# The first three token blocks of a linear-attention and double-MLP kernel in one written order on all engines

## The chip, the cores and the metric

The kernel runs on one core of a Trainium2 chip. The metric is the time of one execution in microseconds on the device. A core has TensorE (PE; PEld is its weight load), VectorE (DVE), ScalarE (ACT), GpSimd (POOL) and SyncE (SP), each with its own queue of instructions that it executes in order. Here SP issues the DMA transfers. A granted clock of 1.00 in the tables is 2.4 GHz on TensorE.

## What is computed

Three layers follow one another: chunked linear attention with decay over 4 sequences of 768 positions and 8 heads, a gated MLP (256 to 1536 to 256) and a second MLP with h times sigmoid(h) (256 to 2048 to 256). The inputs of the MLPs' weights are float64.

```python
for c in range(nc):
    cum = np.cumsum(la, axis=-1)
    L = np.exp(cum[:, :, :, None] - cum[:, :, None, :]) * causal
    M = np.einsum('bhin,bhjn->bhij', Cc, Bc) * L
    y_intra = np.einsum('bhij,bhjd->bhid', M, xc)
    y_inter = np.einsum('bhin,bhnd->bhid', Cc, state) * decay_to_i[:, :, :, None]
    y[:, :, sl] = y_intra + y_inter
    state = decay_full[:, :, None, None] * state + np.sum(Bx, axis=2)
...
gate = 1.0 / (1.0 + np.exp(-(x @ w_gate)))
x1 = gate * (x @ w_val) @ w_out
h = x1 @ w_in
out = (h * (1.0 / (1.0 + np.exp(-h)))) @ w_out2
```

## The kernel before

The 3072 tokens are 24 chunks of 128 positions. A chunk q is sequence q // 6 and place q % 6 (divmod with NCH), so chunks of one sequence stand one behind the other, and each needs the state S of the chunk ahead. The chunks are gathered into seven token blocks, BLOCKS = [2, 2, 4, 4, 4, 4, 4], and the first MLP works block by block.

For a chunk, L is a tile of 128 x 1024 (eight heads) of decays. It is loaded by a DMA that spreads one row over the partitions (at_loadL, L212; for chunk 0 straight from the input, L210) and turned into products of decays by a scan on VectorE (at_L, L295). B and C are loaded as bc; for the first NX = 4 chunks TensorE transposes them (at_wide1), for later ones bf16 pieces are made on GpSimd (L255, L263), ScalarE and VectorE (L280) and transposed by DMA (L284). at_cb multiplies them into PSUM and VectorE takes the product with L (L337). at_y multiplies by x and adds the state's part, at_state and at_state2 (L377, L389) carry the state on with bw (L303) and cw (L308) from GpSimd, and at_yT splits the result into a high and a low part xT (L404, L405).

Weights come as float64, read as pairs of int32. For each of the twelve blocks f of 128 hidden columns, load_w fetches gate, value and output weights (256 KB each), and conv makes float32 out of them: two passes on ScalarE (L136, L137), two on VectorE (L138, L139), an add on GpSimd (L146), then a high part on ScalarE (L147) and a remainder on VectorE (L148). For f < NAT = 7 w_out is first kept whole in a spare place of x1T (L144), used so by the first two blocks, and split later (w1_split, L181 and L182).

A tick (b, f) is a gate product (six matmuls, L462), a sigmoid on ScalarE (L475), a value product (six matmuls), its product with the gate on VectorE (L483) and the output step (L511). In blocks 0 and 1 with f < 7 the output step is two plain float32 products with the whole w_out; everywhere else the gated value is split first (gh on ScalarE, L456; gl on VectorE, L492) and the step has six matmuls. The gate and value products share three PSUM banks (tag gv).

SP's order is written by hand (manual_schedule). The order of the other engines comes from the scheduler of the framework, which simulates the program in the order in which the steps are emitted: slot_steps lists one chunk's steps, and the loop over the ticks mixes them in at an even rate. In the first two blocks the ticks go by groups of GRP = 3 weight blocks, block 0 and block 1 in turn. LAG = 2 output steps stay behind the ticks, across the ends of blocks too. Behind the first MLP follows the second one (L715 to L766), which the change leaves alone but for the rows of the output.

## Time and profile before

| | |
|---|---|
| median of 3 runs (lowest to highest) | 680.84 us (679.74 to 682.12) |
| the profiled execution, its own time | 681.07 us |
| its span, first to last instruction | 679.4 us |
| busy: PE, DVE, ACT, POOL | 647.1, 435.9, 329.3, 106.2 us |
| mean granted TensorE clock | 0.987 |

The times say how long an execution took; the span leaves out what lies around the program's instructions, 1.7 us here. Busy is the time in which an engine executed something, waits that lie inside an instruction among it. The shares over the whole span hide that the stretches differ: the page's row of 40 slices (17 us each) shows PE below 90% in six of the first seven slices and at 90% or more in all but the last of those behind.

### The profile page before, as it was taken

The page shows a single profiled execution, that of the slowest core. Times are in us where ns is not written, and L with a number is a line of the kernel's source. Part 1 is how long each engine was busy: PE and PEld are TensorE (multiplying, and loading weights), DVE is VectorE, ACT ScalarE, POOL GpSimd, SP SyncE. Part 2 cuts the span into 40 slices and gives each one's busy share as a digit, 9 for nine tenths or more (in the row PEclk, how much of TensorE's full clock was granted, in tenths as well). Part 3 has the DMA queues.
Part 4 walks back from the last instruction along what each step waited for, and adds up shares of the span by engine and source line. Part 5 has one row for each costly group of instructions (what it writes and reads, how often), then busy time and mean ns, then how long its engine had stood idle before and what let it go on. Part 6 is the DMA issues. An engine that isn't in the chain of part 4 may idle for free.

```text
span 679.4 us, 10006 instructions
## 1 busy us (share of the span) xinstructions
PE 647.1 (95%) x3728; PEld 524.6 (77%) x3728; DVE 435.9 (64%) x658; ACT 329.3 (48%) x647; POOL 106.2 (16%) x128
## 2 busy tenths in 40 slices
PE   5689788999999999999999999999999999999997
PEld 2368676777777777777787888888888888888887
DVE  8887987766766858656699345464464555644544
ACT  5576634444343644435476334453454444544443
POOL 4545612212121313111133000000000000000000
PEclk9889989999999999999999999999999999999999
DMA  8936568767566375533132000000000000000000
GB/s 204 266 111 182 118 121 152 154 141 129 96 111 141 69 154 119 99 81 116 50 123 77 1 0 1 1 22 10 1 32 1 1 31 1 31 1 1 32 1 31
DMA packets 140144, 51.18 MB, mean 75 GB/s; under 512 B 119008, under 2 KB 133536, under 8 KB 140096
## 3 DMA queue, kind: packets, MB, share of 16 engines
q1 hardware_dynamic: 140096, 50.55, 32.5%
q8 instruction: 29, 0.48, 0.3%
q14 instruction: 19, 0.16, 0.1%
HBM read 36.80 MB, written 3.24 MB: 59 GB/s over the span
## 4 chain that ended last, share of the span: by engine, by line
PE 79%; DVE 7%; DMA 3%; issue 2%; POOL 1%; ACT 1%; SPq 1%; DVEq 0%; ACTq 0%; POOLq 0%
PE h L462 20%; PE acc L511 12%; PE v L462 12%; PE g L462 11%; PE o L740 11%; PE o L751 7%; PE o L746 2%; PE y L352 2%; PE cb L335 1%; DMA raw<-in_moe_w_out_dram 1%; DMA L<-ac_d 1%; DVE cvt L139 1%; DVE L L295 1%; PE y L346 1%; POOL cvt L146 1%
## 5 line engine op out<-in xcount | busy, mean ns | idle before, releaser
L462 PE MATMUL g<-xT,w 128*128 128x512 f32 (+1 forms) x504 | 123.3, 375 | 4.2 <-DVE sg L483 3.8
L462 PE MATMUL v<-xT,w 128*128 128x512 f32 (+1 forms) x504 | 121.6, 373 | 0.2 <-ACT sg L475 0.2
L462 PE MATMUL h<-x2T,w2b 128*128 128x512 f32 x432 | 113.3, 395 | 0.0
L720 DVE TENSOR_TENSOR sh<-h,sh 128x512 f32<-128x512 f32 x96 | 66.4, 691 | 69.5 <-ACT sh L719 69.0
L462 PEld LDWEIGHTS g<-xT,w 128*128 128x128 f32 x504 | 87.7, 191 | 23.4 <-DVE sg L483 4.8
L725 DVE TENSOR_TENSOR gl<-sh,gh 128x512 fp32r<-128x512 f32 x96 | 66.0, 691 | 55.4 <-ACT gh L456 31.8
L462 PEld LDWEIGHTS v<-xT,w 128*128 128x128 f32 x504 | 87.5, 192 | 16.9 <-issue 1.0
L511 PE MATMUL acc<-gh,w 128*128 128x512 f32 (+1 forms) x280 | 96.0, 385 | 1.3 <-ACT x1T L519 1.3
L719 ACT ACTIVATE sh<-h 128x512 f32<-128x512 f32 x96 | 57.7, 601 | 80.7 <-PE h L462 76.1
L456 ACT CAST gh<-sh 128x512 fp32r<-128x512 f32 x96 | 59.2, 620 | 60.1 <-DVE sh L720 53.8
L462 PEld LDWEIGHTS h<-x2T,w2b 128*128 128x128 f32 x432 | 76.5, 188 | 15.2
L456 ACT CAST gh<-sg 128x512 fp32r<-128x512 f32 (+1 forms) x70 | 41.2, 588 | 86.5 <-DVE sg L483 86.4
L740 PE MATMUL o<-w2b,gh 128*128 128x512 f32 x240 | 75.4, 395 | 0.0
L483 DVE TENSOR_TENSOR sg<-v,sg 128x512 f32<-128x512 f32 (+1 forms) x84 | 51.0, 607 | 32.1 <-PE v L462 31.4
L492 DVE TENSOR_TENSOR gl<-sg,gh 128x512 fp32r<-128x512 f32 (+1 forms) x70 | 49.5, 708 | 28.6 <-ACT gh L456 28.3
L475 ACT ACTIVATE sg<-g 128x512 f32<-128x512 f32 (+1 forms) x84 | 45.0, 536 | 37.8 <-PE g L462 34.7
L295 DVE TENSOR_TENSOR_SCAN L<-L,eye 128x1024 f32<-128x1024 f32 x24 | 55.5, 2313 | 10.7 <-DMA L<-ac_d 10.6
L511 PEld LDWEIGHTS acc<-gh,w 128*128 128x128 f32 x280 | 52.5, 191 | 12.6 <-ACT x1T L519 1.8
L751 PE MATMUL o<-w2b,gl 128*128 128x256 f32 x288 | 60.1, 280 | 0.0
L511 PE MATMUL acc<-gl,w 128*128 128x512 f32 (+1 forms) x140 | 54.1, 386 | 4.3 <-DVE gl L492 4.3
L146 POOL TENSOR_TENSOR cvt<-cvt,raw 128x512 int32<-128x512 int32 (+1 forms) x28 | 46.5, 1662 | 67.5 <-DVE cvt L139 47.8
L751 PEld LDWEIGHTS o<-w2b,gl 128*128 128x128 f32 x288 | 49.1, 188 | 4.9
(94 smaller groups left out, 782.0 us busy)
## 6 DMA issues: line engine op xcount, KB each, us to landing
L<-ac_d SPq DMA_DIRECT2D x23, 512.0 KB, 4.6
raw<-in_moe_w_out_dram SPq DMA_DIRECT2D x28, 256.0 KB, 3.6
raw<-in_moe_w_in_dram SPq DMA_DIRECT2D x16, 256.0 KB, 2.7
x<-in_x_dram SPq DMA_DIRECT2D x24, 128.0 KB, 3.0
raw<-in_moe_w_gate_dram SPq DMA_DIRECT2D x12, 256.0 KB, 4.2
raw<-in_moe_w_val_dram SPq DMA_DIRECT2D x12, 256.0 KB, 4.6
out_dram<-o2t SPq DMA_DIRECT2D x24, 128.0 KB, 1.8
bc<-in_B_dram SPq DMA_DIRECT2D x24, 64.0 KB, 2.7
```

Source lines behind the costliest of these rows:

```text
L146: nc.gpsimd.tensor_tensor(ti, ti, r, ALU.add)
L295: nc.vector.tensor_tensor_scan(t["Lf"], t["Lf"], eye, 0.0, op0=ALU.mult, op1=ALU.add)
L456: nc.scalar.copy(hi[:, :n], sg[:, :n])
L462: nc.tensor.matmul(psum[:, :n], w[:, i, o + k * P : o + (k + 1) * P], xt[j][:, k, :n], start=(z == 0), stop=(z == len(k_terms) - 1),)
L483: nc.vector.tensor_mul(sg[:, :n], ps[:, :n], sg[:, :n])
L492: nc.vector.tensor_sub(lo[:, :n], sg[:, :n], hi[:, :n].bitcast(F32))
L511: nc.tensor.matmul(o, v[:, ms], g[:, :n], start=(f == 0 and z == 0 and not (small and m)), stop=(f == NF1 - 1 and z == len(terms) - 1), sk ...
L719: nc.scalar.activation(sg, ps, AF.Sigmoid)
L720: nc.vector.tensor_mul(sg, ps, sg)
L725: nc.vector.tensor_sub(lo, sg, hi.bitcast(F32))
L740: nc.tensor.matmul(ps, hi[:, s], w2(f)[:, :, DM:], start=(f == 0), stop=False, skip_group_check=True,)
L751: nc.tensor.matmul(ps[:, :DM], lo[:, s], w2(f)[:, 0, DM:], start=False, stop=(f == NF2 - 1), skip_group_check=True,)
```

## The change

Chunks are numbered by their place in the sequence: place(q) gives sequence q % 4 and place q // 4, so chunks 0 to 3 are the starts of the four sequences and chunk q takes the state of chunk q - 4. Each sequence has a state tile S2 of its own, and the rows of the output follow the new numbers.

Everything up to the end of block 2 is cut into 657 named steps (a chunk's loads, transposes, scan, products and state; a weight block's seven conversion steps; a tick's five or seven), and a string ORDER lists them. They are emitted in that order with manual_schedule on PE, ACT, DVE and POOL as on SP before. Behind them the scheduler is free again; block 3 begins with no output step left over from block 2. The names: ldw, Af, Ar, D, G, Go, h, l, sh, sl are the weight block's steps, g, sig, v, mul, out (ghi, glo) the tick's, with block and f.

The decays of chunks 0 and 1 no longer come by DMA: all 32 rows' first 128 values are split into two float32r parts, a_hl, and TensorE multiplies them by a column of zeros and ones spread over 128 columns, so that one row lands on all partitions in PSUM (16 matmuls); the scan reads PSUM in two halves.

All twelve weight blocks keep w_out whole for blocks 0 and 1 (SPARE), so no gated value of these two blocks is split. Staging has 3 raw and 3 cvt buffers in place of 4 and 2, bw 2 in place of 1, S 4 in place of 2.

```diff
-NAT = 7
-GRP = 3
+NB = 2
...
+ORDER = """
+aload ldbc.0 ldx.0 aprep ldw.1 arest tp.0 ldL.0 bT.0 dec1 cT1.0 ldw.0 ldL.1 cT0.0 L.0 ldbc.1 Ar.1 cp0.0 ldx.3
...
+cwa.12 ldx.14 cm0.12 cp1.12 cm1.12 st.12 ss.12
+"""
...
-    stg = {"n": 768, "raw": 4, "cvt": 2, "p": sstack.enter_context(tc.tile_pool(name="stg1", bufs=1))}
+    stg = {"n": 768, "raw": 3, "cvt": 3, "p": sstack.enter_context(tc.tile_pool(name="stg1", bufs=1))}
...
+    def place(q):
+
+        return q % nb, q // nb
...
+        steps = [
+            lambda: nc.scalar.activation(f, v[:, :, 1].bitcast(F32), AF.Copy, scale=2.0**-112),
+            lambda: nc.scalar.activation(r, v[:, :, 0].bitcast(U32), AF.Copy, scale=2.0**-29),
+            shift,
+            lambda: nc.gpsimd.tensor_tensor(ti[:, :m], ti[:, :m], r[:, :m], ALU.add),
+            lambda: nc.scalar.copy(hi, f[:, :m]),
+            lambda: nc.vector.tensor_sub(lo, f[:, :m], hi.bitcast(F32)),
+        ]
         if whole is not None:
-            n -= whole.shape[-1]
...
+            steps.append(lambda: nc.gpsimd.tensor_tensor(whole.bitcast(I32), ti[:, m:], r[:, m:], ALU.add))
+        return steps
...
-    whole = lambda f: x1T[0][:, f % 2, NT - (f // 2 + 1) * DM : NT - f // 2 * DM]
...
+    SPARE = [(0, 2048), (1, 2048), (0, 512), (0, 768), (1, 512), (1, 768)]
+    SPARE += [(0, 1024), (0, 1280), (1, 1024), (1, 1280), (0, 1536), (0, 1792)]
+    whole = lambda f: x1T[0][:, SPARE[f][0], SPARE[f][1] : SPARE[f][1] + DM]
...
     def at_loadL(q):
-        b, c = divmod(q, NCH)
+        b, c = place(q)
         t = T[q]
         sl = slice(c * L, (c + 1) * L)
         t["Lf"] = ap_.tile([P, H * L], F32, tag="L", name=f"L{q}", bufs=LB)
         t["L"] = t["Lf"].rearrange("p (h l) -> p h l", h=H)
-        if q == 0:
-            nc.sync.dma_start(out=t["L"], in_=a[b, :, sl].unsqueeze(0).to_broadcast([P, H, L]))
-        else:
-            nc.sync.dma_start(out=t["Lf"], in_=ac_d[c : c + 1, b].to_broadcast([P, H * L]))
+        if q < NB:
+
+            if q == 0:
+                two = ps_acc.tile([P, KM, 512], F32, tag="acc", name=f"a{q}")
+                t["a"] = [two[:, 0], two[:, 1]]
+            else:
+                t["a"] = [ps_at.tile([P, 512], F32, tag=g, name=f"a{q}{g}") for g in ("misc", "cb")]
+            for h in range(H):
+                nc.tensor.matmul(
+                    t["a"][h // 4][:, h % 4 * L : (h % 4 + 1) * L],
+                    pick[:, b * H + h : b * H + h + 1].to_broadcast([2 * U, P]), a_hl,
+                    start=True, stop=True, skip_group_check=True,
+                )
+            return
+        nc.sync.dma_start(
+            out=t["Lf"], in_=ac_d[c : c + 1, b].to_broadcast([P, H * L])
+        )
...
+    def at_L(q):
...
+        if q >= NB:
+            nc.vector.tensor_tensor_scan(t["Lf"], t["Lf"], eye, 0.0, op0=ALU.mult, op1=ALU.add)
             return
...
+        for i in range(2):
+            hs = slice(i * 512, (i + 1) * 512)
+            nc.vector.tensor_tensor_scan(
+                t["Lf"][:, hs], t["a"][i], eye[:, hs], 0.0, op0=ALU.mult, op1=ALU.add
+            )
...
-            if q % NCH:
+            if q >= nb:
                 for m in range(KM):
                     nc.tensor.matmul(
-                        t["y"][:, m], T[q - 1]["S"][:, m * P : (m + 1) * P], t["cwT"],
+                        t["y"][:, m], T[q - nb]["S"][:, m * P : (m + 1) * P], t["cwT"],
...
-    S2 = ap_.tile([P, 2 * D], F32, name="S2")
...
+    S2 = [ap_.tile([P, 2 * D], F32, name=f"S2_{b}") for b in range(nb)]
...
-        add(s + 1, at_state2)
+        add(s - 2, at_state2)
...
-        if b < 2 and f < NAT:
...
+        if b < 2:
...
-        if b >= 2 or f >= NAT:
...
+        if b >= 2 and hi:
+            m1_hi(b, f)
...
+    order = ExitStack()
+    order.enter_context(
+        tc.manual_schedule(
+            engines={
+                mybir.EngineType.PE, mybir.EngineType.Activation,
+                mybir.EngineType.DVE, mybir.EngineType.Pool,
+            }
+        )
+    )
...
+    pick = ap_.tile([2 * U, U], F32R, name="pick")
+    a_hl = ap_.tile([2 * U, L], F32R, name="a_hl")
...
+    def a_prep():
+        clip(a_sb[:, :L])
+        nc.vector.tensor_copy(first[:, 0:1], a_sb[:U, 0:1])
+        nc.vector.memset(a_sb[:, 0:1], 0.0)
+        nc.vector.tensor_copy(a_hl, a_sb[:, :L])
+        nc.vector.tensor_sub(a_hl[U:], a_sb[U:, :L], a_hl[U:].bitcast(F32))
...
+    for k in ORDER.split():
+        plan.pop(k)["fn"]()
+    assert not plan, list(plan)
+    order.close()
...
-            r = b * 512 + t * P
+            i, c = place(b * 4 + t)
+            r = i * S + c * L
...
```

Three places of the order. First VectorE at the start: before, from the clip of chunk 0's decays on (L0, L1 are the decay tiles, cb the products of B and C, cvt and raw a weight block in conversion, e_i and dec the decays for the states).

```order
L201 TENSOR_SCALAR L0_112<-L0_112 128x1024
L558 COPY e_i_155<-ps_e_156 128x192
L295 SCALAR_TENSOR_TENSOR L0_112<-L0_112,eye_97 128x1024
L337 TENSOR_TENSOR L0_112<-cb0_0_164,L0_112 128x512
L567 TENSOR_TENSOR dtmp_197<-ps_e_156,blk_93 128x192
L573 TENSOR_REDUCE dec_199<-dtmp_197 128x24
L138 TENSOR_SCALAR cvt3_201<-cvt3_201 128x768
L139 SCALAR_TENSOR_TENSOR cvt3_201<-raw1_121,cvt3_201 128x768
L337 TENSOR_TENSOR L0_112<-cb0_1_167,L0_112 128x512
L375 COPY S2_104<-st0_188 128x64
L295 SCALAR_TENSOR_TENSOR L1_128<-L1_128,eye_97 128x1024
```

VectorE at the same place after the change, from the scan of the 32 rows for the states on (a0, a1misc and a1cb are the spread decays in PSUM).

```order
L738 SCALAR_TENSOR_TENSOR x1T_81<-x1T_81 32x768
L393 SCALAR_TENSOR_TENSOR L0_141<-a0_142,eye_97 128x512 x2
L393 SCALAR_TENSOR_TENSOR L1_162<-a1misc_163,eye_97 128x512
L393 SCALAR_TENSOR_TENSOR L1_162<-a1cb_164,eye_97 128x512
L186 TENSOR_SCALAR cvt4_192<-cvt4_192 128x768
L187 SCALAR_TENSOR_TENSOR cvt4_192<-raw2_158,cvt4_192 128x768
L459 TENSOR_TENSOR L0_141<-cb0_1_198,L0_141 128x512
L459 TENSOR_TENSOR L0_141<-cb0_0_184,L0_141 128x512
L186 TENSOR_SCALAR cvt3_182<-cvt3_182 128x768
L187 SCALAR_TENSOR_TENSOR cvt3_182<-raw1_131,cvt3_182 128x768
```

The scans of chunks 0 and 1 stand one behind the other now, ahead of the first weight conversion, and the second conversion follows the first with only two products between.

Then ScalarE between chunk 1's transposes and the results of the first two chunks (xT0 is the high part of a result y, w1 the converted weights): before, where the second weight block's conversion stands behind the first result.

```order
L243 COPY bT1_173<-bcT1_170 128x128
L247 ACTIVATE x1T_81<-bcT1_170,blk_93 128x128 x8
L404 CAST xT0_0_243<-y0_231 128x2x128
L319 COPY cwT1_249<-cwT1_247 128x128
L181 CAST w1_103<-x1T_81 128x256
L147 CAST w1_103<-cvt3_201 128x512
L136 ACTIVATE cvt5_281<-raw2_132 128x768
L137 ACTIVATE raw2_132<-raw2_132 128x768
L404 CAST xT0_0_243<-y1_259 128x2x128
```

ScalarE at the same place after the change.

```order
L321 COPY bT1_224<-bcT1_214 128x128
L328 ACTIVATE x1T_81<-bcT1_214,blk_93 128x128 x8
L193 ACTIVATE raw5_217<-raw5_217 128x768
L192 ACTIVATE cvt6_253<-raw5_217 128x768
L542 CAST xT0_0_274<-y0_232 128x2x128
L196 CAST w1_103<-cvt3_182 128x512
L196 CAST w1_103<-cvt4_192 128x512
L542 CAST xT0_0_274<-y1_291 128x2x128
```

The conversion of the third weight block (raw5) moved ahead of both results and of the high parts of the first two weight blocks.

Last VectorE in block 2, ticks 2 and 3 (sg the gated values, gl their remainders, L9 to L14 decay tiles of later chunks): before.

```order
L483 TENSOR_TENSOR sg2_2_1502<-v2_2_1512,sg2_2_1502 128x512
L280 COPY st010_1457<-bc310_1442 128x8x32
L280 COPY st110_1475<-bc310_1442 128x8x2x16
L295 SCALAR_TENSOR_TENSOR L10_1065<-L10_1065,eye_97 128x1024
L337 TENSOR_TENSOR L9_972<-cb9_0_1396,L9_972 128x512
L377 SCALAR_TENSOR_TENSOR S2_104<-S2_104,dec_199,st9_1489 128x64
L405 TENSOR_TENSOR xT1_3_1454<-y8_1402,xT0_3_1453 128x2x128
L492 TENSOR_TENSOR gl2_2_1521<-sg2_2_1502,gh2_2_1520 128x512
L389 TENSOR_TENSOR S9_1504<-S2_104,blk_93 128x256
L483 TENSOR_TENSOR sg2_3_1572<-v2_3_1577,sg2_3_1572 128x512
```

VectorE there after the change, from the product of tick 1 on.

```order
L642 TENSOR_TENSOR sg2_1_1390<-v2_1_1397,sg2_1_1390 128x512
L363 COPY st110_1410<-bc310_1356 128x8x2x16
L654 TENSOR_TENSOR gl2_1_1424<-sg2_1_1390,gh2_1_1423 128x512
L389 SCALAR_TENSOR_TENSOR L9_1408<-L9_1408,eye_97 128x1024
L363 COPY st010_1438<-bc310_1356 128x8x32
L389 SCALAR_TENSOR_TENSOR L10_1426<-L10_1426,eye_97 128x1024
L642 TENSOR_TENSOR sg2_2_1436<-v2_2_1429,sg2_2_1436 128x512
L389 SCALAR_TENSOR_TENSOR L14_1442<-L14_1442,eye_97 128x1024
L514 SCALAR_TENSOR_TENSOR S2_1_105<-S2_1_105,dec_116,st9_1464 128x64
L389 SCALAR_TENSOR_TENSOR L11_1459<-L11_1459,eye_97 128x1024
L514 SCALAR_TENSOR_TENSOR S2_0_104<-S2_0_104,dec_116,st8_1497 128x64
L642 TENSOR_TENSOR sg2_3_1469<-v2_3_1471,sg2_3_1469 128x512
```

Where one scan stood between two ticks, four stand between tick 1 and tick 3, and the scan of chunk 14, which the list does not hold, was set among them by the scheduler.

## Rows read from the trace of the kernel before

**Rows 1.** Windows by stage: busy us (instructions) per engine, granted clock, DMA share, GB/s.

```profile
0.00:26.40 26.40, 15.11 (x89) 7.19 (x89) 22.23 (x32) 15.70 (x41) 10.23 (x22) 0.90 0.86 209
26.40:119.50 93.10, 77.24 (x610) 64.99 (x608) 77.00 (x116) 50.75 (x114) 38.37 (x36) 0.94 0.65 152
119.50:181.00 61.50, 61.50 (x381) 46.95 (x381) 42.83 (x67) 28.55 (x62) 13.57 (x24) 0.99 0.70 134
181.00:679.40 498.40, 493.29 (x2655) 405.50 (x2653) 293.81 (x445) 234.32 (x431) 44.00 (x47) 1.00 0.19 47
```

**Rows 2.** VectorE's waits, 26.4 to 119.5 us: us in total, times, longest.

```profile
DVE cvt L138 <- ACT cvt L136: 3.4, 3, 2.1
```

**Rows 3.** VectorE's groups, 26.4 to 119.5 us: busy us, mean ns | idle before.

```profile
L483 DVE TENSOR_TENSOR sg<-v,sg 128x256 f32<-128x256 f32 x24 | 10.0, 415 | 2.0 <-PE v L462 2.0
L337 DVE TENSOR_TENSOR L<-cb,L 128x512 f32<-128x512 f32 x12 | 8.2, 684 | 3.8 <-PE cb L329 3.0 <-PE cb L335 0.8
...
L182 DVE TENSOR_TENSOR w<-x1T,w 128x256 fp32r<-128x256 f32 x6 | 6.2, 1027 | 0.0
L148 DVE TENSOR_TENSOR w<-cvt,w 128x512 fp32r<-128x512 f32 x6 | 5.1, 850 | 0.4 <-ACT w L147 0.4
...
L405 DVE TENSOR_TENSOR xT<-y,xT 128x256 fp32r<-128x256 f32 x6 | 2.5, 419 | 0.7 <-ACT xT L404 0.7
L377 DVE SCALAR_TENSOR_TENSOR S<-S,dec,st 128x64 f32<-128x64 f32 x4 | 1.1, 277 | 1.6 <-PE st L368 1.6
```

**Rows 4.** Lines of VectorE, 0 to 190 us: shortest/median/longest ns, first and last start.

```profile
L138 DVE TENSOR_SCALAR cvt<-cvt x12: 545/552/1178, 11.9 to 81.1; 128x768 int32<-128x768 int32 x12
L139 DVE SCALAR_TENSOR_TENSOR cvt<-raw,cvt x12: 942/955/1158, 12.5 to 83.1; 128x768 int32<-128x768 int32 x12
L148 DVE TENSOR_TENSOR w<-cvt,w x12: 681/943/2335, 20.0 to 90.8; 128x512 fp32r<-128x512 f32 x7, 128x768 fp32r<-128x768 f32 x5
L182 DVE TENSOR_TENSOR w<-x1T,w x7: 416/892/1525, 19.1 to 57.5; 128x256 fp32r<-128x256 f32 x7
L389 DVE TENSOR_TENSOR S<-S,blk x12: 400/424/1458, 16.4 to 186.7; 128x256 f32<-128x256 f32 x12
L280 DVE COPY st<-bc x24: 194/220/1877, 72.1 to 180.4; 128x256 bf16<-128x256 bf16 x24
```

**Rows 5.** Timeline near 30 us: start, duration in us, engine, line.

```profile
30.24 2.28 DVE L295 TENSOR_TENSOR_SCAN L<-L,eye 128x1024 f32<-128x1024 f32 x1
...
30.45 2.59 POOL L144 TENSOR_TENSOR x1T<-cvt,raw 128x256 int32<-128x256 int32 x1 [2.34 <-DMA raw<-in_moe_w_out_dram]
...
33.01 1.48 POOL L146 TENSOR_TENSOR cvt<-cvt,raw 128x512 int32<-128x512 int32 x1
```

**Rows 6.** Lines of GpSimd, 0 to 190 us: shortest/median/longest ns.

```profile
L144 POOL TENSOR_TENSOR x1T<-cvt,raw x7: 727/927/2594, 13.6 to 56.3; 128x256 int32<-128x256 int32 x7
...
L255 POOL TENSOR_TENSOR bcr<-bc x12: 614/615/1422, 69.0 to 178.4; 128x256 f32<-128x256 f32 x12
...
L303 POOL TENSOR_TENSOR bw<-bc,L x13: 412/446/1180, 10.2 to 184.2; 128x128 f32<-128x128 f32 x13
```

**Rows 7.** Timeline of the opening: first weight conversion, an f32 product, the first gate's run.

```profile
10.60 0.91 ACT L136 ACTIVATE cvt<-raw 128x768 f32<-128x768 f32 x1 [3.06 <-DMA raw<-in_moe_w_out_dram]
...
25.29 2.07 PE L329 MATMUL cb<-x1T,bT 128*128 128x512 f32 x2
...
26.37 1.98 PE L462 MATMUL g<-xT,w 128*128 128x256 f32 x5
```

**Rows 8.** TensorE's timeline: tick 11 of block 2, first gates of blocks 3 and 4.

```profile
172.97 1.56 PE L462 MATMUL g<-xT,w 128*128 128x512 f32 x6
174.37 1.56 PE L462 MATMUL v<-xT,w 128*128 128x512 f32 x6
...
178.19 1.65 PE L462 MATMUL g<-xT,w 128*128 128x512 f32 x6
...
237.34 1.65 PE L462 MATMUL g<-xT,w 128*128 128x512 f32 x6
```

More of the change, by code (lines that the diff above doesn't have):

```diff
@@ L228, in at_load_x @@
     def at_load_x(q):
-        b, c = divmod(q, NCH)
+        b, c = place(q)
         t = T[q]
@@ L398, in at_yT, with at_yT_lo, x_alloc @@
         if i == 0:
+            x_alloc(b)
+        nc.scalar.copy(xT[b][0][:, :, i * L : (i + 1) * L], t["y"])
+    def at_yT_lo(q):
+        b, i = blk_of[q]
+        hi, lo = (v[:, :, i * L : (i + 1) * L] for v in xT[b])
+        nc.vector.tensor_sub(lo, T[q]["y"], hi.bitcast(F32))
+    def x_alloc(b):
+        if b != 1:
             xT[b] = [
@@ L515, in m1_out, with m1_x1 @@
                 )
-        if f == NF1 - 1:
-            for m in range(KM):
-                o = a_[:, m * n : (m + 1) * n] if small else a_[:, m, :n]
-                nc.scalar.copy(x1T[0][:, m, start_of[b] : start_of[b] + n], o)
+        if f == NF1 - 1 and to_x1:
+            m1_x1(b)
+    def m1_x1(b):
+        n = BLOCKS[b] * L
+        small = n <= 256
+        a_ = acc[b - b % 2][:, b % 2] if small else acc[b]
+        for m in range(KM):
+            o = a_[:, m * n : (m + 1) * n] if small else a_[:, m, :n]
+            nc.scalar.copy(x1T[0][:, m, start_of[b] : start_of[b] + n], o)
@@ L607, in tile_linattn_moe_moe @@
-    ticks = [(b, f) for fs in GR for b in (0, 1) for f in fs]
-    seen.add(("w", 0))
-    seen.add(("x", 0))
-    for b in range(2, len(BLOCKS)):
-        ticks += [(b, f) for f in range(NF1)]
+    scr = lambda k, i, n=U: x1T[0][:n, k, i * S : (i + 1) * S]
+    order = ExitStack()
[5 more added lines that the diff above has]
+            }
+        )
+    )
@@ new lines, in decays1, with decays2, decays3, decays4 @@
+    def decays1():
+        nc.vector.tensor_tensor_scan(first, a_sb[:U], first, 0.0, op0=ALU.mult, op1=ALU.add)
+    def decays2():
+        T[0]["e"] = ps = ps_at.tile([P, 512], F32, tag="misc", name="ps_e")
+        for c in range(NCH):
+            nc.tensor.transpose(
+                ps[:, c * U : (c + 1) * U], first[:, c * L : (c + 1) * L], ident[:U, :U]
+            )
+    def decays3():
+        nc.vector.tensor_copy(e_i.rearrange("p c u -> p (c u)"), T[0]["e"][:, : NCH * U])
+    def decays4():
+        T[0]["d"] = ps = ps_at.tile([P, 512], F32, tag="misc", name="ps_d")
+        nc.tensor.matmul(
+            ps[:, : NCH * U], sel, e_i.rearrange("p c u -> p (c u)"), start=True, stop=True
+        )
@@ L613, in tile_linattn_moe_moe @@
+    step("dec4", "PE", 0.64, decays4, after=["dec3"], takes=[("misc", 1, ["dec5"])], lag=0.2, group="d")
+    step("dec5", "DVE", 0.72, decays5, after=["dec4"], lock=True, group="d")
+    for q in range(ends[PB] + 3):
+        plan_chunk(q, 5 if q < ends[PB] else 2 - q + ends[PB])
+    for f in range(NF1):
+        plan_weights(f)
+    for b in range(PB):
+        for f in range(NF1):
+            plan_tick(b, f)
+    ticks = [(b, f) for b in range(PB, len(BLOCKS)) for f in range(NF1)]
     w2st = {}
@@ L616, in run @@
         for _ in range(min(k, len(steps))):
-            steps.pop(0)()
-    def need(k):
-        while k not in seen:
             steps.pop(0)()
```

532 lines of the change are left out of this document (354 added, 178 removed).

## The prediction

> **What bounds the kernel now.** I read the windows by stage first. The trace falls into four stretches [rows 1]: an opening up to 26.4 us, the first two token blocks up to 119.5 us, the third block up to 181.0 us, and the rest. In the third block TensorE is busy for all of its 61.50 us and in the rest for 493.29 of 498.40 us, so there nothing but less matmul work would help. The second stretch is different: TensorE has 77.24 us of work in 93.10 us, and VectorE is busy for 77.00 us. So the order can gain in one place: what the 93.1 us are made of.
>
> VectorE's time there has three parts. The groups of lines [rows 3] and the shortest durations [rows 4] give the first two. With the groups that read SBUF twice at their shortest duration and the others, of fourteen, at their mean, count by count, VectorE needs 62.9 us (for instance 6 x 0.416 us for the w_out remainder at L182 that took 6.2 us, 6 x 0.681 us for L148 that took 5.1 us). The other 14.1 us of its 77.0 busy us are stretch. The last 16.1 us are idle, put down to other engines' late results; the largest is a wait for a weight conversion on ScalarE [rows 2].
>
> The stretch has a visible cause. In rows 5 a scan on VectorE starts at 30.24 us and a GpSimd add starts 0.21 us later; the add ends at 33.04 us, 0.52 us after the scan, though such an add takes 0.73 us otherwise [rows 6]. On VectorE the operations with two SBUF inputs reach up to nine times their shortest duration (L182 1.525 for 0.416, L280 1.877 for 0.194) [rows 4], while L337 and L483, which read PSUM, keep 684 and 415 ns as means [rows 3]. So the two engines take turns wherever VectorE reads SBUF twice, and about 0.2 us of a turn is hidden at the hand-over.
>
> **The opening: no gain.** The decays of the first two chunks are now spread by TensorE instead of by DMA. That is 16 matmuls of 128 columns. No row shows this form. Bounds: 0.06 us each, a quarter of the 0.23 us that a 512-column one takes in rows 8, and 0.26 us, a quarter of the f32 product at 25.29 us (2.07 us for two) [rows 7]. That is 1 to 4 us in all; I take 2.5. VectorE has the clips and a 32-row scan to do meanwhile, so it is covered. The scans of chunks 0 and 1 can then run one behind the other from about 6.5 us.
>
> What holds the first gate is data. The weight conversion in rows 7 starts on ScalarE at 10.60 us, when the DMA lands, and 1.77 MB were issued up to that transfer. In the new order of SP the second weight block issued (f = 0, the first one used), the third and x of chunk 1 stand at 2.03, 3.57 and 4.23 MB (weight blocks of 0.79 MB, L tiles of 0.52, x and bc of 0.13 each, a and its copy of 0.10). With the 209 GB/s of the opening [rows 1] they land 1.2, 8.6 and 11.8 us later, at 11.8, 19.2 and 22.4 us. On ScalarE the two conversions of the third block (0.91 us each) stand ahead of the small copies that the first gate needs, as the order of ScalarE above shows: 19.2 + 1.8 + about 1.6 for three copies, an estimate of half a conversion each, is 22.6 us. VectorE then does one remainder (0.68), the scan of chunk 2 (2.28) and two short ones (0.7): 26.3 us. Before, the first gate's run begins at 26.37 us [rows 7]. I put both at 26.4.
>
> **The first two blocks: the term that decides.** In the new order VectorE has, between the first gate and the first gate of block 2, 10 conversions (0.545 + 0.942), 6 scans (2.28), 12 products with the decays (0.684), 11 remainders (0.681), 24 value products (0.415), 11 remainders of w_out (0.416), 12 copies for the transposes (0.194), 5 state products (0.400), 6 remainders of xT (0.419) and 6 state sums (0.277): 14.9 + 13.7 + 8.2 + 7.5 + 10.0 + 4.6 + 2.3 + 2.0 + 2.5 + 1.7 = 67.4 us at the shortest durations [rows 3 to 5]. It was 62.9. All twelve weight blocks now keep w_out whole at first; that takes ten splits of the gated values off ScalarE and VectorE, and adds five more GpSimd adds and splits of w_out. GpSimd's work there is 10 adds of 512 columns (1.48) [rows 5], 10 of 256 (0.73), 14 of bc (0.614) and 13 of bw and cw (0.412) [rows 6]: 36.1 us. TensorE has some 64 us of work and is not the bound.
>
> To 67.4 us come stretch and idle, 30.2 us before. The new order fixes all engines' queues so that chunks of four sequences alternate and no chunk waits for the state of the one just ahead. I expect a third of the idle, 5.5 us. GpSimd's 36.1 us must share with 45 us of two-input work (14.9 + 13.7 + 7.5 + 4.6 + 2.3 + 2.0); it can lie beside the other 22 us, which read PSUM, so I take 9 us of stretch, two thirds of what it was. That makes 82 us, from both sides: 73 (81 us of turns less 0.2 us at each of 37 hand-overs, nothing idle) and 97.6 (67.4 + 30.2).
>
> By the Trainium skill, "SBUF — State Buffer", section "Who interferes with whom", a VectorE instruction with two SBUF inputs and a GpSimd instruction that reads SBUF exclude each other for the whole instruction, and VectorE work on PSUM excludes nothing; rows 4 and 5 agree, but for the 0.2 us. It speaks against the change in so far as this stretch would then have a floor of 45 + 36 = 81 us whatever the order, and the total one of 670 us; that would rule out (c) below and make (a) the likeliest.
>
> **Block 2.** The next block of the same 12 ticks and four chunks ran from 178.19 to 237.34 us, 59.15 us, with no idle on TensorE; block 2 itself took 61.5 [rows 1, 8]. I take 60. A piece of VectorE's order costs more: four scans, 9.1 us, stand within seven instructions, one of them (L14) belonging to block 3 and moved up by the scheduler, which is free behind the fixed order (last order above). From the product of tick 1 to that of tick 3 VectorE has some 13 us of work, and the first scan waits about 1 us for its DMA; TensorE has 8 groups of 1.40 us [rows 8] and two small ones, 11.8 us, before it needs the bank that this product frees. So about 2.5 us of stall, 0 to 4.8: 62.5 us.
>
> **The rest** stays at 498.4 us. Both orders enter block 3 with chunks up to 11 done; the new one has finished two output steps (1.40 us each) more, which is why I count the old block 2 to 181.0, not to 178.19. The scheduler is free again there, and TensorE has no gap to give back [rows 1].
>
> **The sum.** 26.4 + 82 + 62.5 + 498.4 = 669.3 us of span, against 26.4 + 93.1 + 61.5 + 498.4 = 679.4. The profiled execution took 681.07 us with that span, so 1.7 us lie around it: 671.0 us. It stands 0.2 us above the median of the runs, which I leave in.
>
> **Rivals.** (a) Turns are strict and idle comes on top: 81 + 5.5 = 86.5 us, so 675.5 us. For it: the scan in rows 5 makes GpSimd wait to its end, and scans are 13.7 us of this stretch. (b) The slower side: fixed queues pack no better than the scheduler's. One late transfer or one stretched add then holds every instruction behind it on its engine, and the first blocks keep the old 30.2 us of stretch and idle on 67.4 us of work: 97.6 us, 686.6 us. It decides as soon as stretch and idle together are over about 25 us. For it: GpSimd's work in this stretch grows by some 4 us; against it: the waits of rows 2 are 2.1 us at the longest and come from other chunks' work, which the new order separates. (c) Everything fits: 73 us and no stall in block 2 (60), 659.5 us. (d) The fixed order does little: stretch and idle shrink by a third only, 87.5 us, and block 2 stalls the full 4.8 us; 678.8 us, and about no change with a late opening on top.
>
> **How the numbers follow.** Chances: my forecast, 664 to 675 us, 0.53; (a) 0.16; (b) 0.13; (c) 0.10; (d) 0.08. The range leaves out (b) above and the far end of (c) below: 657 to 683 us. A difference under 0.3% (2 us) can't be told from none. Faster takes the forecast, (a), (c) and a little of (d): 0.81. Same takes most of (d): 0.07. Slower is (b): 0.12.
>
> **What would show it.** In the changed profile the first long run of gate matmuls should begin near 26 us, the first 512-column gate near 108 us, the first gate of block 3 near 171 us, and the stretch behind it should last 498 us. VectorE should be busy over 90% from 26 to 108 us, and L182's successor should still show stretched copies. A 512-column gate before 102 us means turns cost less than I think; one after 118 us means (b). A block 3 that starts over 66 us after block 2 means that the scans in a row cost more than a bank. The prediction falls if the last stretch is not 498 us, since everything in it is counted as unchanged.

## The result: 1.25% slower

The changed kernel takes 689.75 us, median of four executions from 685.54 to 691.02, against 680.86 us: ratio 1.0125, 95% interval 1.0099 to 1.0151. The forecast was 671.0 us. The profiled execution took 690.01 us with a span of 688.3 us, so 1.7 us lie around it as before.

The windows by stage of the changed kernel answer to [rows 1]; the columns are the same, the borders are its own first gates (27.28, 119.02 and 181.27 us).

```profile
0.00:27.28 27.28, 17.54 (x87) 9.54 (x87) 19.70 (x34) 12.74 (x30) 7.77 (x18) 1.00 0.87 214
27.28:119.02 91.74, 79.60 (x597) 66.51 (x596) 70.10 (x115) 50.56 (x118) 43.49 (x48) 0.96 0.69 145
119.02:181.27 62.25, 57.59 (x328) 44.11 (x327) 39.68 (x59) 24.64 (x54) 12.01 (x15) 0.95 0.53 104
181.27:688.30 507.03, 503.22 (x2718) 409.39 (x2716) 295.42 (x455) 237.66 (x441) 42.15 (x52) 1.00 0.20 48
```

The first two blocks last 91.74 us: hardly anything is won there, though VectorE is busy for 70.10 us in place of 77.00. Block 2 has a hole: TensorE is busy for 57.59 of 62.25 us, at a granted clock of 0.95. The last stretch is 507.03 us long and not 498.40, with TensorE busy nearly throughout. (Counted from its own first gate of block 3, at 178.19 us in [rows 8], the kernel before takes 501.2 us.)

VectorE's groups in the first two blocks answer to [rows 3] (busy us, mean ns, idle before it and what ended that):

```profile
L389 DVE TENSOR_TENSOR_SCAN L<-L,eye 128x1024 f32<-128x1024 f32 x7 | 17.5, 2494 | 1.8 <-DMA L<-ac_d 1.8
...
L197 DVE TENSOR_TENSOR w<-cvt,w 128x512 fp32r<-128x512 f32 x11 | 9.0, 828 | 4.8 <-ACT w L196 4.8
...
L237 DVE TENSOR_TENSOR w<-x1T,w 128x256 fp32r<-128x256 f32 x11 | 5.8, 537 | 1.6 <-ACT w L235 1.6
...
L363 DVE COPY st<-bc 128x256 bf16<-128x256 bf16 x12 | 2.5, 216 | 2.0 <-DMA tr<-st 2.0
```

Most of the stretch did go: the w_out remainder, 1027 ns in [rows 3], is at 537, and its shortest in [rows 4] is 416. What came in its place shows in the waits of ScalarE in that stretch (us in total, times, longest):

```profile
ACT st L363 <- DMA tr<-st: 12.7, 7, 3.1
ACT sg L633 <- PE g L614: 10.6, 11, 3.3
ACT w L196 <- POOL cvt L195: 6.4, 5, 2.4
ACT cvt L192 <- DMA raw<-in_moe_w_out_dram: 3.5, 2, 2.2
```

The largest is a wait for a transfer. The stacks st that are transposed by DMA have one buffer each, so ScalarE's copy into a stack waits until the transfer of the stack before it has landed. ScalarE executes its row in order, so the sigmoids and weight conversions behind the copy wait too. The chain of waits says the same. On the page of the changed kernel its line by engine is

```profile
PE 80%; DMA 9%; DVE 3%; SPq 3%; ACT 2%; issue 2%; POOL 1%; ACTq 0%; DVEq 0%; POOLq 0%
```

where the kernel before had DVE 7% and DMA 3%. The chain through block 2's worst place (start us, us, what):

```profile
117.67 3.30 DMA tr<-st
...
121.35 0.93 ACT st L363 x2
122.28 0.50 ACT sg L633
122.78 0.30 ACT w L235
123.08 0.65 SPq L380
...
125.15 5.72 DMA L<-ac_d
...
130.90 2.30 DVE L L389
133.20 0.07 issue
133.27 2.45 POOL bw L406
135.72 0.04 issue
135.76 0.44 PE st L498 x8
```

It reads: a transpose lands late, ScalarE is held, SyncE issues the loads of L late, they need 5.72 us, then come a scan and a multiplication on GpSimd, and for that TensorE stops with the state matmuls of chunk 9. The windows around it (granted clock third from the end) show what the stop costs:

```profile
128.00:132.00 4.00, 4.00 (x19) 3.15 (x17) 1.80 (x2) 1.97 (x5) 0.00 (x0) 1.00 0.91 298
132.00:136.00 4.00, 0.54 (x10) 0.20 (x8) 4.00 (x4) 0.60 (x1) 2.44 (x1) 0.79 0.41 168
136.00:140.00 4.00, 4.00 (x17) 3.10 (x10) 4.00 (x4) 0.62 (x1) 2.12 (x1) 0.50 0.10 10
140.00:144.00 4.00, 4.00 (x22) 2.90 (x22) 1.49 (x4) 0.00 (x0) 0.41 (x1) 0.86 0.24 23
```

TensorE stands still for 3.5 us there, and behind that its clock is at the lower level (0.50 is 1.2 GHz) for a whole window of 4 us and a part of the next (0.86), which takes away some 2.6 us more (0.50 of the first 4 us and 0.14 of the next 4).

### The profile page after: what moved, and what is told of

Read it like the earlier page. It is cut to its first block, busy times and chain, and to the rows that moved or that the text cites. A ratio compares the mean times of both kernels' runs of the same rounds, so it can differ in the third digit from the quotient of the medians.

```text
span 688.3 us, 9969 instructions
## 1 busy us (share of the span) xinstructions
PE 658.0 (96%) x3724; PEld 529.5 (77%) x3724; DVE 424.9 (62%) x660; ACT 325.6 (47%) x642; POOL 105.4 (15%) x132
## 4 chain that ended last, share of the span: by engine, by line
PE 80%; DMA 9%; DVE 3%; SPq 3%; ACT 2%; issue 2%; POOL 1%; ACTq 0%; DVEq 0%; POOLq 0%
PE h L614 19%; PE acc L673 12%; PE v L614 12%; PE g L614 12%; PE o L1056 11%; PE o L1067 7%; DMA tr<-st 5%; PE o L1062 2%; PE y L474 1%; DVE L L389 1%; DMA raw<-in_moe_w_out_dram 1%; PE cb L453 1%; PE y L468 1%; DMA raw<-in_moe_w_gate_dram 1%; SPq L211 1%
## 5 line engine op out<-in xcount | busy, mean ns | idle before, releaser
L614 PE MATMUL g<-xT,w 128*128 128x512 f32 (+1 forms) x504 | 122.7, 376 | 5.1 <-ACT sg L633 1.9
L614 PE MATMUL v<-xT,w 128*128 128x512 f32 (+1 forms) x504 | 121.8, 377 | 2.2 <-ACT sg L633 2.1
L614 PE MATMUL h<-x2T,w2b 128*128 128x512 f32 x432 | 113.3, 395 | 0.0
L1036 DVE TENSOR_TENSOR sh<-h,sh 128x512 f32<-128x512 f32 x96 | 66.3, 690 | 69.6 <-ACT sh L1035 69.1
L614 PEld LDWEIGHTS g<-xT,w 128*128 128x128 f32 x504 | 87.4, 193 | 23.9 <-DVE xT L547 2.3
L614 PEld LDWEIGHTS v<-xT,w 128*128 128x128 f32 x504 | 86.8, 193 | 19.3 <-ACT sg L633 3.2
L614 PEld LDWEIGHTS h<-x2T,w2b 128*128 128x128 f32 x432 | 76.5, 188 | 15.2
L673 PE MATMUL acc<-gh,w 128*128 128x512 f32 x240 | 87.0, 403 | 0.0
L608 ACT CAST gh<-sg 128x512 fp32r<-128x512 f32 x60 | 37.2, 620 | 78.6 <-DVE sg L642 75.2
L642 DVE TENSOR_TENSOR sg<-v,sg 128x512 f32<-128x512 f32 (+1 forms) x84 | 50.9, 606 | 30.7 <-PE v L614 28.3
L654 DVE TENSOR_TENSOR gl<-sg,gh 128x512 fp32r<-128x512 f32 x60 | 44.3, 739 | 23.8 <-ACT gh L608 23.5
L389 DVE TENSOR_TENSOR_SCAN L<-L,eye 128x1024 f32<-128x1024 f32 x22 | 51.9, 2360 | 11.0 <-DMA L<-ac_d 11.0
L195 POOL TENSOR_TENSOR cvt<-cvt,raw 128x512 int32<-128x512 int32 x28 | 43.8, 1563 | 96.1 <-DVE cvt L187 54.2
L673 PEld LDWEIGHTS acc<-gh,w 128*128 128x128 f32 x240 | 45.6, 191 | 11.2 <-issue 0.6
L1056 PEld LDWEIGHTS o<-w2b,gh 128*128 128x128 f32 x240 | 45.1, 188 | 8.5
```

The lines of the kernel that those rows point to most:

```text
L389: nc.vector.tensor_tensor_scan(t["Lf"], t["Lf"], eye, 0.0, op0=ALU.mult, op1=ALU.add)
L608: nc.scalar.copy(hi[:, :n], sg[:, :n])
L614: nc.tensor.matmul(psum[:, :n], w[:, i, o + k * P : o + (k + 1) * P], xt[j][:, k, :n], start=(z == 0), stop=(z == len(k_terms) - 1),)
L642: nc.vector.tensor_mul(sg[:, :n], ps, sg[:, :n])
L654: nc.vector.tensor_sub(lo[:, :n], sg[:, :n], hi[:, :n].bitcast(F32))
L673: nc.tensor.matmul(o, v[:, ms], g[:, :n], start=(f == 0 and z == 0 and not (small and m)), stop=(f == NF1 - 1 and z == len(terms) - 1), sk ...
```

## The experiments

The theory after these rows, **A**: the rows of the order were drawn up with transfers landing too early. The changed kernel's table of steps still carries the figures, though the running code doesn't use them:

```python
add("ldL", "SP", 2.0, lambda: at_loadL(q), after=["astore"], lag=1.6,
...
add(f"tr{w}", "SP", 1.5, lambda w=w: at_bc3t(q, w),
    after=[n(f"sd{w}"), n(f"sb{w}")], takes=[(f"tr{w}", 2, [n("cp1")])], lag=1.6)
```

A load of L is to land 3.6 us after its issue begins; on the page of the changed kernel the median is 5.3 us. A transpose is to land after 3.1 us; up to 200 us the median is 3.6 us and the longest takes 5.3. Rivals: **B**, VectorE's work sets the stage as in the prediction; **C**, the staging buffers for raw weights (three for four); **D**, the numbering by place.

**The order lifted.** The four engines are ordered by the scheduler again.

```diff
     order = ExitStack()
-    order.enter_context(
-        tc.manual_schedule(
-            engines={
-                mybir.EngineType.PE, mybir.EngineType.Activation,
-                mybir.EngineType.DVE, mybir.EngineType.Pool,
-            }
-        )
-    )
```

> Edit: the explicit order is lifted from TensorE, VectorE, ScalarE and GpSimd (SyncE keeps it), so those four engines are ordered again as in the kernel before; numbering by place, spread matmuls, list of steps and buffers stay. Theory A (the fixed rows hold a queue behind a transfer that lands later than the planner's 1.6 us: 4.3 to 7.2 us for the loads of L, 3.1 to 5.3 us for the transposes): the 4 us gap of TensorE at 132 us is gone or shorter, first two blocks plus block 2 take 148 us or less (154.0 with the order), total 684 us or less. Rival B (the numbering by place and the new stages cost it, whatever the order): those stages stay at 154 us or more, total 688 us or more.

Measured: 705.86 us, ratio 1.0372 (1.0320 to 1.0423). The first 512-column gate came at 134.8 us. So with everything else of the change in place, the explicit order, poor as it is, is worth about 16 us over the scheduler's. (SyncE keeps the list's order here, and the scheduler gets the steps in the list's sequence; whether another sequence would have served it better was not tried.) Theory A in the form "the order loses the time" is wrong: the rest of the change loses more, and the order wins back a part.

**Chunk 9's state step later, two stack buffers, and both.**

```diff
-glo.2.1 v.2.2 sig.2.2 sb0.10 L.9 ldL.14 out.2.0 g.2.3 sd0.10 ldL.11 bw.9 L.10 st.9 sig.2.3 v.2.3 mul.2.2
-out.2.1 ss.9 ghi.2.2 L.11 g.2.4 st.8 v.2.4 ss.8 bw.10 mul.2.3 bw.11 ldbc.14 glo.2.2 ghi.2.3 cwp.10 g.2.5
+glo.2.1 v.2.2 sig.2.2 sb0.10 L.9 ldL.14 out.2.0 g.2.3 sd0.10 ldL.11 bw.9 L.10 sig.2.3 v.2.3 mul.2.2
+out.2.1 st.9 ss.9 ghi.2.2 L.11 g.2.4 st.8 v.2.4 ss.8 bw.10 mul.2.3 bw.11 ldbc.14 glo.2.2 ghi.2.3 cwp.10 g.2.5
```

```diff
-        t["stk", which] = ap_.tile([P, H, 8, N], BF16, tag=f"st{which}", name=f"st{which}{q}", bufs=1)
+        t["stk", which] = ap_.tile([P, H, 8, N], BF16, tag=f"st{which}", name=f"st{which}{q}", bufs=2)
```

> Edit: one step, the state matmuls of chunk 9 and what adds them up, stands two groups of TensorE (v.2.3 and out.2.1, 2.8 us) later in the order; nothing else. Theory A: the wait on GpSimd at 132 us falls from 3.5 us to 1 or 2 us, the granted clock in the 4 us behind it stays at or near 1.00 (0.50 with the change), and both come off the end: about 684 us (2.5 us of wait and 2.9 us of clock less). Rival B (the work is only shifted and the wait comes back at the next row): 688 us or more, the clock falls again.

> Edit: two buffers for each of the two stacks that are transposed by DMA (one before); to make room two small tiles lie in buffers that are free at that time. Theory A (from 93 to 121 us each stack waits for the transfer of the one before, five chunks of some 5 us in a chain): ScalarE's waits in front of the stacks fall from 12.7 us in the first two blocks and 7.0 us in block 2 to below 4 us each; the first 512-column gate comes at 113 to 115 us (119.0 with the change), total 683 to 686 us. Rival B (VectorE's work and its shared turns set the stage, as in the prediction): the gate stays at 118 to 119.5 us and the total at 689 us.

> Edit: both of the two earlier edits, the state matmuls of chunk 9 two groups later and two buffers for each stack. If the two losses are separate (a stop in block 2 worth 3.5 us, a chain of transfers in the first two blocks worth 2.5 us), they add up: 683 to 684 us. If they are one loss seen twice (the scans of chunks 9, 10, 14 and 11 in a row), the two together give no more than the better one: 685.5 to 686.5 us. In both cases slower than the kernel before.

Measured: 686.22 us (ratio 1.0086, 1.0067 to 1.0104), 687.18 (1.0110, 1.0080 to 1.0139) and 685.58 (1.0070, 1.0040 to 1.0100). With the state step two groups later the stop is broken into short ones and the clock holds (windows of that run):

```profile
132.00:136.00 4.00, 3.24 (x21) 2.19 (x20) 4.00 (x5) 0.78 (x2) 2.72 (x2) 1.00 0.31 127
136.00:140.00 4.00, 3.19 (x20) 1.92 (x18) 4.00 (x3) 0.21 (x1) 1.96 (x1) 1.00 0.22 21
```

That gave 3 of the 5 us expected. The two stack buffers did away with the 12.7 us that ScalarE waited for transposes in the first two blocks (none is listed any more), and the stage became only 2.4 us shorter (89.29 us; the first 512-column gate at 116.87 us, where 113 to 115 was expected). ScalarE's waits there, in that run:

```profile
ACT sg L633 <- PE g L614: 15.0, 14, 3.1
ACT w L196 <- POOL cvt L195: 8.0, 5, 2.4
ACT cvt L192 <- DMA raw<-in_moe_w_out_dram: 3.9, 3, 2.4
```

Other waits took most of the place. The two edits together give little more than the better one. So neither of these two waits costs the 19 us that the forecast missed; with one removed, others came in its place.

**The same buffers in the kernel before.** There the order is the scheduler's.

> Edit: the same two buffers for each stack, in the kernel before the change. Theory A (the chain of transfers is held by the fixed rows): without fixed rows the buffer is worth little, 679 to 681.5 us. Rival B (a chain of transposes bounds both kernels alike): 675 us or less here too.

Measured: 681.10 us, ratio 1.0014 (0.9989 to 1.0040), no difference: in the scheduler's order the single buffer costs nothing.

**Raw buffers, both ways.** Four in the changed kernel, three in the kernel before.

```diff
-    stg = {"n": 768, "raw": 3, "cvt": 3,
+    stg = {"n": 768, "raw": 4, "cvt": 3,
```

```diff
-    stg = {"n": 768, "raw": 4, "cvt": 2,
+    stg = {"n": 768, "raw": 3, "cvt": 3,
```

> Edit: four staging buffers for the raw weights in the first MLP, as the kernel before has them (the change has three); small tiles lie in buffers that are free at that time, to make room. Order unchanged. Theory C (the first two blocks wait for weights: with the change SyncE waits 20.7 us in front of weight loads for GpSimd to empty a raw buffer, and the chain of waits passes two of those loads between 71 and 85 us): those waits fall below 8 us, the first 512-column gate comes at 112 to 115 us (119.0 with the change), total 683 to 686 us. Rival B (VectorE's work and latencies between engines set the stage, loads have slack): the gate stays at 118 us or later, total 688 us or more.

> Edit of the kernel before: three raw staging buffers and three of the converted ones, as the changed kernel has them (before: four and two). Theory C (raw buffers bound the first two blocks): 684 us or more, the first 512-column gate 3 us or more behind 119.5 us. Rival B: 679 to 682 us.

Measured: 688.84 us for the changed kernel with four (ratio 1.0123, no gain), 687.67 for the kernel before with three and three (1.0099, 1.0067 to 1.0131). In the scheduler's order three raw and three converted buffers cost 7 us over four and two. In the explicit order a fourth one is hardly used: SyncE's row puts the loads where three allow them, and its waits in front of weight loads for GpSimd only fell from 20.7 to 14.7 us, while those for VectorE in front of the loads of L rose from 6.7 to 11.4.

**The numbering alone**, in the kernel before.

```diff
-        b, c = divmod(q, NCH)
+        b, c = place(q)
...
-                        t["y"][:, m], T[q - 1]["S"][:, m * P : (m + 1) * P], t["cwT"],
+                        t["y"][:, m], T[q - nb]["S"][:, m * P : (m + 1) * P], t["cwT"],
...
-        t["S"] = ap_.tile([P, DM], F32, tag="S", name=f"S{q}", bufs=2)
+        t["S"] = ap_.tile([P, DM], F32, tag="S", name=f"S{q}", bufs=5)
```

> Edit of the kernel before: only the numbering of chunks by place (four sequences in turn, state tiles kept for five chunks, outputs stored accordingly); its own order, staging and decays. Theory D (the numbering is what makes the changed kernel slow without its explicit order, 705.9 us): 690 us or more. Rival E (the numbering is neutral or helps, since a chunk's state is needed four chunks later, not one; the rest of the change costs it): 676 to 682 us.

Measured: 685.63 us, ratio 1.0074 (1.0050 to 1.0098), between the two expectations. Numbering and raw buffers thus cost 5 and 7 us under the scheduler. If they add, they explain about half of the 25 us by which the changed kernel without its order stands behind the kernel before. The other half (spread decays, whole w_out, the sequence in which the steps are emitted) was not taken apart.

**The scan of chunk 14.** The list doesn't name it, and the scheduler set it between the scans of chunks 10 and 11. Here it is a step at the list's end.

> Edit: the scan of chunk 14 (2.3 us of VectorE, for block 3), which stands between the scans of chunks 10 and 11 in the changed kernel although the explicit order doesn't name it, is put behind the order's last step; nothing else. If it costs the order what it takes (L.11, the state step of chunk 9 and the products behind them come 2.3 us later): 686 to 687.5 us. If the stop at 132 us is due to the scan of chunk 9 alone, which stands ahead of it: 688.5 to 690 us.

Measured: 690.52 us, ratio 1.0145 (1.0108 to 1.0182). It costs nothing there; TensorE still waits 3.7 us for bw of chunk 9.

**Other orders of the same steps.** If the rows are at fault and not the steps, another list must do better. Lists were drawn up by moving single steps, or a few neighbours, to other places at random and keeping what brought TensorE's last step earlier, in a small model where each engine executes its row in order. All moves keep the steps, their dependencies and the buffers of the changed kernel; the scan of chunk 14 is a step here too. First with figures taken from its trace:

```diff
-aload ldbc.0 ldx.0 aprep ldw.1 arest tp.0 ldL.0 bT.0 dec1 cT1.0 ldw.0 ldL.1 cT0.0 L.0 ldbc.1 Ar.1 cp0.0 ldx.3
+aload aprep ldL.1 arest ldbc.0 dec1 ldw.0 tp.0 L.1 bT.0 ldbc.1 ldL.0 bw.1 ldw.1 cT0.0 L.0 cT1.0 Af.0 Ar.0 bw.0 tp.1
...
+    step("L.14", "DVE", 2.35, lambda: at_L(14), after=["ldL.14"])
```

> Edit: the same 657 steps (and the scan of chunk 14 as a 658th) in another order, drawn up again with what the trace of the changed kernel shows in place of the planner's figures: 3.4 to 5.6 us from the issue of a transfer to its landing, transfers one behind the other on the 16 engines, GpSimd held while VectorE scans or splits weights (the 12 integer additions took 3.1 us, planned 1.35), steps behind a matmul 0.2 us later. Work, buffers and staging are those of the changed kernel. Theory A (the rows were drawn up with transfers and GpSimd too fast, and each late one holds a whole queue): the first 512-column gate comes at 96 to 108 us (119.0 with the change), that of block 3 at 160 to 172 us (181.3), total 665 to 680 us. Rival B (the rows are as good as such rows can be, the rest is work and hand-overs that none of them shows): 686 us or more.

Measured: 665.21 us, ratio 0.9773 (0.9739 to 0.9807): 24 us faster than the changed kernel and 16 faster than the kernel before. Its windows by stage (borders at its own first gates):

```profile
0.00:32.37 32.37, 20.97 (x101) 10.92 (x101) 28.92 (x42) 18.70 (x46) 12.23 (x23) 0.88 0.90 220
32.37:100.91 68.54, 67.88 (x576) 59.97 (x574) 60.98 (x97) 41.26 (x94) 34.71 (x40) 0.98 0.88 196
100.91:159.62 58.71, 58.71 (x374) 45.52 (x372) 42.75 (x72) 25.53 (x58) 9.80 (x16) 1.00 0.50 89
159.62:663.58 503.96, 499.47 (x2684) 407.75 (x2681) 295.48 (x451) 239.09 (x444) 43.38 (x53) 1.00 0.21 49
```

Its opening is longer and has more of the work in it. The first 512-column gate comes at 100.9 us, 18 us earlier, and TensorE is busy for 67.88 of 68.54 us ahead of it and all through block 2. On its page the chain of waits reads

```profile
PE 93%; DVE 3%; DMA 1%; SPq 1%; issue 1%; DVEq 0%
```

The expectation of this run has one figure wrong: it puts the 512-column adds on GpSimd at 3.1 us. Of the ten in the first two blocks of the changed kernel (shortest, median and longest in ns) three took that long and seven 1.29:

```profile
L195 POOL TENSOR_TENSOR cvt<-cvt,raw x10: 1287/1297/3292, 34.3 to 95.2; 128x512 int32<-128x512 int32 x10
```

The model itself used 1.3 us and held GpSimd while VectorE does certain work; no run shows what that one figure is worth.

What was better in that list, the figures or the search? Four more lists, the same search each time.

> Edit: the same 658 steps in an order drawn up by the same search, but with the planner's own figures (durations of the changed kernel's table, 1.6 us from the end of an issue to the landing, turns between GpSimd and VectorE without loss). Theory A (the figures are at fault): little is won over the changed kernel's rows, 682 to 689 us. Rival S (the search is at fault: with the same figures a better order was to be had): 665 to 672 us, next to the order drawn with measured figures (665.2). Both at fault: 673 to 681 us.

> Edit: as the last, with one group of figures measured: transfers land 3.4 to 5.6 us behind their issue and one behind the other; GpSimd's steps keep the planner's durations. If the landings are the figure that matters: 665 to 670 us. If GpSimd's are: no better than with the planner's figures alone.

> Edit: as e11, with the other group measured: GpSimd held while VectorE scans or splits (and all engines' durations from the trace); transfers land 1.6 us behind their issue. If GpSimd's figures matter: 665 to 670 us. If the landings do: no better than with the planner's figures alone.

> Edit: a second, independent draw of the order with all measured figures, which has hardly a stretch in common with the first. Theory A: 663 to 669 us, the first 512-column gate at 94 to 104 us; what orders drawn alike differ by is then the measure for the three other runs. If the first draw was luck: over 672 us.

| list drawn with | us, median | ratio (95%) | first gate of block 2, us |
|---|---|---|---|
| measured figures, first draw | 665.21 | 0.9773 (0.9739 to 0.9807) | 100.9 |
| measured figures, second draw | 664.35 | 0.9761 (0.9733 to 0.9789) | 101.3 |
| the table's own figures | 675.93 | 0.9919 (0.9885 to 0.9952) | 111.4 |
| landings measured only | 683.33 | 1.0035 (1.0016 to 1.0053) | 101.5 |
| GpSimd and engines' durations only | 678.76 | 0.9973 (0.9955 to 0.9990) | 105.4 |

The two draws with all measured figures lie 0.9 us apart, though their lists differ from the first line on. With the table's own figures the search finds an order 14 us better than the changed kernel's: so over half of the 24 us lies in how the list was drawn from its figures, not in the figures. The lists with all measured figures are 11 us better still. Which group of them matters for the total can't be told: with one alone the lists came out no better than with none, so each of the two runs points at the other's group. In the first two blocks, where the forecast failed most, either group alone brought block 2's first gate forward (table above). The list with landings alone has that stretch done as early as the best ones and then stops twice in block 2 (the last line is the window of that block):

```profile
PE y L465 <- DVE xT L544: 5.9, 1, 5.9
PE g L612 <- DVE sg L640: 4.2, 1, 4.2
...
101.52:175.75 74.23, 64.15 (x373) 48.46 (x371) 42.71 (x68) 27.98 (x63) 15.96 (x19) 0.93 0.42 79
```

(L465, L544, L612 and L640 are L468, L547, L614 and L642 of the changed kernel.) Two stops, 10.1 us, and the clock behind them (0.93) make block 2 last 74.2 us and not 58.7: a few badly placed rows lose most of the gain of the others. For the three lower lines there is one draw each, so a few us of their differences may be the draw.

## Why the prediction was wrong

The forecast was 19.0 us low (690.0 against 671.0), 7 us outside its range, and of the wrong sign. The sum shows where:

| term | forecast | measured | off by |
|---|---|---|---|
| opening, to the first gate | 26.4 | 27.3 | +0.9 |
| first two blocks | 82 | 91.7 | +9.7 |
| block 2, with all its output steps | 62.5 | 66.3 | +3.8 |
| the rest | 498.4 | 503.0 | +4.6 |

Seventeen of block 2's 72 output matmuls stood behind block 3's first gate, so 17 x 0.234 = 4.0 us are counted to block 2 in this table (62.3 + 4.0) and taken off the rest (507.0 - 4.0). The opening is counted here to the first gate matmul; the forecast's 26.4 was the begin of the run of gate matmuls, which came at 29.45 us. By that border the opening is 3.1 us late and the first two blocks 7.5 us.

**The opening.** The steps were right: data holds the first gate. The 16 spread matmuls are within their bounds (3.7 us from the first start to the last end), but the first scan began at 7.59 us and not at 6.5. The third weight block was ready for ScalarE at 22.53 us and not at 19.2:

```profile
22.53 0.88 ACT L193 ACTIVATE raw<-raw 128x768 int32<-128x768 uint32 x1 [5.89 <-DMA raw<-in_moe_w_out_dram]
...
27.28 0.56 PE L614 MATMUL g<-xT,w 128*128 128x256 f32 x1
...
29.45 0.79 PE L614 MATMUL g<-xT,w 128*128 128x256 f32 x2 [1.61 <-DVE xT L547]
```

Of these 3.3 us the first gate's first matmul took 0.9, and its next ones waited for xT up to 29.45 us; that part is counted to the next term.

**The first two blocks: the step that failed is the idle term.** The sum was 67.4 us of VectorE work + 9 of stretch + 5.5 of idle. VectorE was idle for 91.74 - 70.10 = 21.6 us, four times the forecast and more than the 16.1 before. Its busy 70.1 us hide two errors that nearly cancel. The durations of its twelve groups in this stretch add up to 76.8 us, of which 69.9 by the forecast's durations (one more scan than counted), so the stretch was 6.9 us, not 9. But records of neighbouring instructions overlap, and busy time counts the overlap once: 6.7 us here (76.8 against 70.1), 6.9 in the kernel before, whose fourteen groups add up to 83.9 us against 77.0 busy. The 62.9 us of the kernel before are net of it (with 14.1 of stretch they make the 77.0 busy us), the 67.4 that were compared to them are not: added up like these, the kernel before needs about 70 us, so VectorE's work did not grow. I had argued that no chunk waits for another's state any more. That held, but states were not what it now waited for: its largest waits are for weight conversions on ScalarE (4.8 and 2.6 us), and ScalarE waited 18.8 us for transfers. How much of the 21.6 us goes back to transfers no run shows; that the order of the steps made it is shown by the lists that changed nothing else (VectorE idle for 7.6 us in the first draw's stretch, 9.4 in the second's). Stretch and idle came to 24.3 us, and rival (b) named both the mechanism ("one late transfer ... holds every instruction behind it on its engine") and the point from which it decides, some 25 us; its sign, a 512-column gate after 118 us, came true too. Its 97.6 us for this stretch did not, and the total passed its 686.6 us only by what block 2 and the rest added. At 0.13 I gave it far too little. Its case needed the landing times, and I had them; I used them for the opening alone.

By the Trainium skill, "SBUF — State Buffer", section "Who interferes with whom", a VectorE instruction with two SBUF inputs and a GpSimd instruction that reads SBUF exclude each other; the first two blocks would so have had a floor of 81 us by the forecast's count. The changed kernel is 10 us above it, so that floor wasn't what bound it. In the second draw, with some splits moved out of that stretch, the same count at the shortest durations (1.29 us for a 512-column add, not 1.48) gives 72 us (39.4 of two-input work on VectorE, 32.7 on GpSimd) and the stage lasts 74.7:

```profile
26.60:101.31 74.71, 70.76 (x585) 61.21 (x586) 65.34 (x104) 44.08 (x99) 44.58 (x44) 1.00 0.84 190
```

The trace agrees with the rule in so far as the stage is no shorter. Which of the two is nearer to binding there, the turns or TensorE with its 70.8 busy us, isn't shown.

**Block 2.** Four scans in a row stall TensorE: right as to the place, in part as to the cause, not as to the path and the size. I priced the wait of a PSUM bank at 2.5 us, at most 4.8. The stop of 3.46 us came at the state matmuls of chunk 9: the loads of L were issued at 125.2 us behind a late transpose, and the multiplication for bw stood beside the second scan of the row and took 2.44 us in place of 0.41, so by an estimate from these two numbers 2.0 of the 3.46 us go back to the scans in a row. The forecast had no term for the clock, which took another 2.6 us.

**The rest.** "Stays at 498.4 us" failed, and it was the step on which I said the prediction falls. From block 3's first gate it is 507.0 us, 507.0 in the two runs with one edit, 507.0 with four raw buffers and 507.1 with both edits, so it comes with the order and not with a disturbance. From gate to gate the kernel before takes 501.2 us (679.4 - 178.2), so 5.8 us are to be explained. TensorE idles early and is the bound late, so work that is moved back costs its full time, and three things moved.

First, the free scheduler puts block 3's first gates (181.27 us) ahead of the order's last out steps, whose last remainder starts on VectorE at 182.06 us: the changed kernel has 17 output matmuls left, the one before 12, and "no output step left over", in the description of the change, is true of the list alone.

Second, "both orders enter block 3 with chunks up to 11 done" was misread. The kernel before has chunk 12's products done too, a chunk without a state product; the 16 matmuls stand just ahead of its gate:

```profile
177.26 0.65 PE L352 MATMUL y<-L,x 128*32 128x128 f32 x16
```

So the changed kernel has 16 more products with x left, 12 more of B and C (eight of chunk 12, four of chunk 13) and four more state products, which chunk 12 has in the new numbering.

Third, in the new numbering no chunk behind the gate is without a state product, in the old one chunk 18 is: four more. The run with the numbering alone gives its price: 502.3 us from gate to gate, 1.1 more than the kernel before.

Taken from the start of each such matmul to the start of the next, the outputs take 2.2 us more than before, the products with x 1.7, the state products 1.3, those of B and C 1.0; all others together 0.4 less (in the kernel before TensorE stands still for 1.3 us at 365 us, in the changed one not). That is the whole 5.8 us.

What the forecast had right is what the steps allow. An order of these steps (and of chunk 14's scan, which cost nothing by itself) can bring block 2's first gate to 101 us (forecast 108) and the total to 664 us. The forecast's error was to take the list in the change for such an order; it never set the list's planned landings beside the measured ones.

## What to carry to other kernels

A fixed order on in-order engines is only as good as the landing times and durations it was drawn up with and the search behind it; before trusting one, take the landing times from the trace, set them beside the lags it assumes, and ask what stands behind each instruction that waits for a transfer. Removing the longest wait tells little when many chains are nearly as long: two edits that each removed a visible wait gave 4 us of 24. And when an engine idles early and bounds late, count how much of its work a renumbering moves across that border.
